# Windowed attention decode beside an MLP, one core: V streamed 256 columns at a time past masked P, exp written in 16-key runs, fewer idle products

## The chip, the core and the metric

The kernel runs on one core of a Trainium2 chip. The metric is the device time of one execution in microseconds (us); lower is better. The kernel before measures 216.69 us (median of 4 runs, 216.23 to 217.12). A profile's span is about 1.3 us shorter than the time of the same run.

## The reference, cut to what matters

One decoding step for 4 sequences: the output is the sum of the input, windowed attention over a cache, and a small MLP.

```python
# A: attention; 32 query heads, 16 kv heads, head width 128
W = min(4096, max(256, Sk // 4))                 # 2048 keys
q = (xn @ wq) ...                                # x is [4, 1, 576]
k, v = last W keys of k_cache, v_cache           # [4, 16, 2048, 128] each, bf16
p = softmax(q k^T * Dh**-0.5);  o = p v
attn = o @ wo                                    # wo [4096, 576]
# B: MLP
h  = gelu(layernorm(xn) @ w1);  x1 = xn + shift(h) @ w2
h2 = gelu(layernorm(x1) @ w3) @ w4               # w3 [576, 4608], w4 [4608, 576]
return x + attn + x1 + h2
```

K and V are 33.6 MB each, the weights 21.4 MB more. 88.49 MB have to come from HBM, and every byte of the cache is used once.

## The kernel before: the parts that matter

The program is written as lists of instructions for each engine with explicit semaphores. One queue issues all large loads in order: weights, 16 K pieces of 2 MB, 8 V pieces of 4 MB into four buffers, then wo, then w4 in five pieces. V piece 4 may be issued only when piece 0 has been used, and so on.

```python
v_free = [["hT1", "hs1", "h2_3"], ["h2_3"], [t_done(NC - 3)], [t_done(NC - 1)]]
for c in range(8):                               # V pieces
    add_dma([(vslot[q], ...)], ("v", q), [f"PV{c - 4}_3"] if b else v_free[q], KS + c)
ev_wo = add_dma(..., "wo", ["PV4_3"], KS + 8)
# w4: five pieces of 18, 9, 6, 2, 1 rows, waiting for PV5_3 (two) and PV6_3 (three)
```

After the K stage, exp computes P and writes its results one after the other to places that lie 64 elements apart (the layout of P itself stays the same in the change; only the order in which exp goes through it differs); P is transposed by products with selection matrices; VectorE multiplies it with a 0/1 mask into "pads" of 64 columns; and V is the *stationary* operand of each product:

```python
P_exp = P_sb.rearrange("p (i q t) -> p q t i", i=NI, q=4)     # innermost step: 64 elements
... activation(out=P_exp[:, q], in_=Sps[:, q, :].rearrange("p (t i) -> p t i", t=16), func=Exp, ...)

def pe_PV(c, j):                                 # a quarter of V piece c: 32 products of 64 columns
    for t in range(VQ):
        e.matmul(OTps, lhsT=vt[:, VQ * j + t, :], rhs=pads[:, j, t].rearrange("p h e -> p (h e)"), ...)
```

The V products stand in a loop of two passes (pieces 0 to 3, then 4 to 7), so that their instructions exist once. HOPS puts a jump at a chosen place inside the loop. IDLE puts products of zeros at three places of TensorE's program near the end: 3 before the permutation of the attention output, 7 after the wo products, 5 after the first w4 piece.

```python
IDLE = ((3, -2.7), (7, 0.5), (5, 20.5))
HOPS = (("K", 15), ("V", 5))
```

## Time and profile before

| | before |
|---|---|
| span of the profiled run | 215.7 us (that run took 217.06, the median is 216.69) |
| loads | 88.49 MB, DMA row full from slice 2 to 38 |
| TensorE busy | 153.5 us, mean granted clock 0.913 |
| one V piece on TensorE | 128 products, 3.9 us (full clock) to 5.4 us |
| one exp (128 x 512) | 2.76 us, four of them |
| last load landed | 211.59 us; end of the last product about 213.85 us |
| instruction fetches | 10, of 16 KB each |

DMA, the sixteen engines that move the loads, is the resource that is never free, and TensorE's chain after the wo load ends 2.3 us later than the last load. One line of the page counts the packets of the queue that fetches instructions (packets, MB, share of 16 engines):

```profile
q8 instruction: 10, 0.16, 0.3%
```

### The profile page before, as it was taken

How to read it: one execution, taken by the hardware profiler on the slowest of the kernel's cores; microseconds unless marked ns; L12 is line 12 of the kernel's file. 1: busy time of each engine (PE TensorE's matmuls, PEld its weight loads, DVE VectorE, ACT ScalarE, POOL GpSimd, SP SyncE). 2: the span in 40 equal slices, each digit the busy share in tenths (PEclk: the TensorE clock that was granted, in tenths of full speed). 3: DMA queues.
4: the chain of work that ended last, by engine and by line, in shares of the span. 5: the costliest groups of instructions: out<-in, count | busy, mean ns of one | idle time of the engine just before them, and what ended most of it. 6: DMA issues, size and time to landing. Idle time of an engine off the chain costs nothing. (4 is left out here: it accounts for less than half of the span.)

```text
span 215.7 us, 5968 instructions
## 1 busy us (share of the span) xinstructions
PE 153.5 (71%) x2688; PEld 118.5 (55%) x2691; DVE 104.4 (48%) x160; ACT 67.9 (31%) x74; POOL 15.5 (7%) x55
## 2 busy tenths in 40 slices
PE   0048499999999999999993009597566718380996
PEld 0023176777888788877882003587555718370553
DVE  0242522676666667666665111999679716110000
ACT  2001205655566666665565882000000000000000
POOL 8200000710000000000000000000000000000000
PEclk9999969999999999999999556999799967888599
DMA  7999999999999999999999999999999999999970
GB/s 292 402 404 462 437 407 425 422 427 422 428 434 425 422 434 425 433 428 425 441 431 444 431 437 428 425 434 422 437 416 444 413 456 413 447 410 429 405 317 5
DMA packets 5152, 88.68 MB, mean 411 GB/s; under 512 B 600, under 2 KB 740, under 8 KB 1300
## 3 DMA queue, kind: packets, MB, share of 16 engines
q1 hardware_dynamic: 5124, 88.49, 96.2%
q8 instruction: 10, 0.16, 0.3%
q14 instruction: 2, 0.02, 0.0%
q10 hardware_dynamic: 16, 0.01, 0.0%
HBM read 88.49 MB, written 0.00 MB: 410 GB/s over the span
## 5 line engine op out<-in xcount | busy, mean ns | idle before, releaser
L365 DVE COPY kt<-ps 128x1024 bf16<-128x1024 bf16 x80 | 52.3, 687 | 27.4 <-PE ps L358 27.2
L358 PE MATMUL ps<-perm_bf,ring 128*128 128x128 bf16 x1024 | 62.4, 219 | 1.6 <-PEq L607 0.6
L358 PEld LDWEIGHTS ps<-perm_bf,ring 128*128 128x128 bf16 x1024 | 57.5, 98 | 10.9 <-issue 10.8
L364 ACT ACTIVATE kt<-ps 128x1024 bf16<-128x1024 bf16 x48 | 49.1, 1024 | 31.1 <-PE ps L358 29.8
L436 DVE TENSOR_TENSOR kt<-PT,mU_bf 128x2048 bf16<-128x2048 bf16 x32 | 37.1, 1217 | 10.3 <-PE ps L447 10.1
L447 PE MATMUL ps<-kt,ring 128*128 128x64 bf16 x512 | 20.2, 211 | 14.5 <-PEq L607 10.2
L447 PEld LDWEIGHTS ps<-kt,ring 128*128 128x128 bf16 x512 | 19.7, 110 | 14.9 <-issue 14.9
L584 ACT ACTIVATE out_sb<-ps 4x288 bf16<-4x288 f32 x1 | 0.4, 402 | 79.6 <-PE ps L465 79.6
L447 PE MATMUL ps<-kt,w 128*128 128x64 bf16 x512 | 16.3, 193 | 7.0 <-PEq L607 5.8
L447 PEld LDWEIGHTS ps<-kt,w 128*128 128x128 bf16 x512 | 15.5, 98 | 7.8 <-issue 7.4
L372 PE MATMUL ps<-kt,Qs 128*32 128x512 bf16 x272 | 17.8, 382 | 1.4 <-PEq L607 1.4
L411 PE MATMUL ps<-kt,sel 128*128 128x512 bf16 x16 | 5.5, 516 | 12.2 <-ACT kt L403 12.2
L465 PE MATMUL ps<-w,ORT 128*4 128x288 bf16 x64 | 6.6, 392 | 5.9 <-DMA w<-in_A_wo_dram 5.9
L411 PEld LDWEIGHTS ps<-kt,sel 128*128 128x128 bf16 x16 | 1.9, 124 | 15.8 <-ACT kt L403 12.7
L393 POOL COPY Qs<-Qpad 128x128 bf16<-128x128 bf16 x16 | 4.6, 296 | 81.8 <-PE ps L372 67.4
L294 PE MATMUL ps<-ident_bf,xn_bf 4*128 4x4 bf16 x8 | 0.6, 170 | 13.7 <-DVE ragsrc L288 13.7
L583 DVE CAST out_sb<-ps 4x288 bf16<-4x288 f32 x1 | 0.4, 445 | 20.2 <-PE ps L465 20.2
L403 ACT ACTIVATE kt<-ps,negb 128x512 bf16<-128x512 f32 x4 | 9.4, 2702 | 2.6 <-DVE negb L400 2.6
L372 PEld LDWEIGHTS ps<-kt,Qs 128*32 128x32 bf16 x272 | 5.7, 95 | 6.8 <-issue 1.5
L465 PEld LDWEIGHTS ps<-w,ORT 128*4 128x4 bf16 x64 | 3.9, 115 | 8.4 <-issue 6.0
L294 PEld LDWEIGHTS ps<-ident_bf,xn_bf 4*128 4x128 bf16 x8 | 0.4, 112 | 13.8 <-issue 11.4
L278 ACT ACTIVATE sd<-mv 4x1 f32<-4x1 f32 x3 | 0.6, 202 | 16.2 <-DVE mv L276 16.2
(108 smaller groups left out, 81.2 us busy)
## 6 DMA issues: line engine op xcount, KB each, us to landing
ring<-in_A_k_cache_dram SPq DMA_DIRECT2D x16, 2048.0 KB, 14.4
w<-in_A_v_cache_dram SPq DMA_DIRECT2D x4, 4096.0 KB, 22.0
ring<-in_A_v_cache_dram SPq DMA_DIRECT2D x4, 4096.0 KB, 29.9
w<-in_B_w_dram SPq DMA_DIRECT2D x1, 4608.0 KB, 24.0
w<-in_A_wo_dram SPq DMA_DIRECT2D x1, 4608.0 KB, 34.0
kt<-in_A_wq_dram SPq DMA_DIRECT2D x1, 4096.0 KB, 13.1
w<-in_B_w_dram SPq DMA_DIRECT2D x1, 2592.0 KB, 33.8
w<-in_B_w_dram SPq DMA_DIRECT2D x3, 576.0 KB, 14.1
```

The lines of the kernel that those rows point to most:

```text
L278: add("act", lambda e: e.activation(out=sd[:, idx:idx + 1], in_=mv[:, idx, 1:2], func=ACTF.Sqrt, bias=EPS, scale=1.0), waits=[f"{tag}_mv"] ...
L294: e.transpose(XTps[idx][:, r, :], v[:, r, :], ident_bf[0:B, 0:B])
L358: ins = e.transpose(tb[n % 4][:, t, :], slot_t(c)[:, 8 * k + t, :], perm_bf[:])
L364: return "act", lambda e: e.activation(out=ktbuf[:, n % 16], in_=tb[n % 4], func=ACTF.Copy)
L365: return "dve", lambda e: e.tensor_copy(out=ktbuf[:, n % 16], in_=tb[n % 4])
L372: ins = e.matmul(Sps[32 * u:32 * u + 32, q, :].rearrange("p (t i) -> p t i", t=16), lhsT=Qs[:, c % NPOS, 32 * u:32 * u + 32], rhs=ktgrp[:, ...
L393: P(lambda e, c=c, cc=cc: e.tensor_copy(out=Qs[:, c % NPOS, :], in_=Qpad_t[:, 128 * cc:128 * cc + 128]), waits=["qT", "qs_zero"] + ([f"SC{ ...
L403: add("act", lambda e, q=q: e.activation(out=P_exp[:, q], in_=Sps[:, q, :].rearrange("p (t i) -> p t i", t=16), func=ACTF.Exp, bias=negb[: ...
L411: ins = e.matmul(ps[:, 4 + g, :].rearrange("p (q t) -> p q t", q=4), lhsT=sel[:, g // 2, g % 2, i, :], rhs=P_v[:, i], start=(i == 0), stop ...
L436: return lambda e: e.tensor_tensor(out=pads[:, j], in0=PTv[:, b, q, VQ * j:VQ * (j + 1), :].unsqueeze(2).to_broadcast([128, VQ, 32, 2]), i ...
L447: ins = e.matmul(OTps, lhsT=vt[:, VQ * j + t, :], rhs=pads[:, j, t].rearrange("p h e -> p (h e)"), start=(q == 0 and j == 0 and t == 0), s ...
L465: return e.matmul(ACC[h], lhsT=lhsT, rhs=rhs, start=start, stop=stop, tile_position=(0, 32 * h), skip_group_check=True)
```

## The change

Its intent is to give TensorE longer products in the V stage, which have less overhead and keep its clock up, and then to do without most of the idle products. Now masked P is the stationary operand (two pads side by side: 128 columns) and two V tiles of 128 columns move past it. Half of each 128 x 256 result is meaningless; the two diagonal blocks are copied out to fp32 and summed by products with a folding matrix. exp writes 16 keys next to each other. (The last lines of this diff tell the code in short.)

```diff
-IDLE = ((3, -2.7), (7, 0.5), (5, 20.5))
-HOPS = (("K", 15), ("V", 5))
+IDLE = ((3, -2.7),)
+HOPS = (("K", 15), ("V", 11))
-        P_exp = P_sb.rearrange("p (i q t) -> p q t i", i=NI, q=4)
+        P_exp = P_sb.rearrange("p (i q t) -> p q i t", i=NI, q=4)
-   activation(out=P_exp[:, q], in_=Sps[:, q, :].rearrange("p (t i) -> p t i", t=16), func=ACTF.Exp,
+   activation(out=P_exp[:, q], in_=Sps[:, q, :].rearrange("p (t i) -> p i t", t=16), func=ACTF.Exp,
...
-                for t in range(VQ):
-                    ins = e.matmul(OTps, lhsT=vt[:, VQ * j + t, :], rhs=pads[:, j, t].rearrange("p h e -> p (h e)"), ...)
+                for t in range(0, VQ, 2):
+                    t0 = (VQ * j + t) * Dh
+                    ins = e.matmul(Ops, lhsT=pads[:, j, t:t + 2].rearrange("p t h e -> p (t h e)"), rhs=vslot[q][:, t0:t0 + 2 * Dh], ...)
...
-   after piece 3 and 7: OTn[:, cols] = OTps * rinvB[:, cols]                      (VectorE)
+   after piece 3 and 7: Ov[0:64, b] = Ops[0:64, 0:128]       (VectorE)
+                        Ov[64:128, b] = Ops[64:128, 128:256] (ScalarE)
+   def pe_fold: for b in 0, 1: OTps[:, 64*b:64*b+64] = Ov[:, b, :]^T fold_f       (TensorE, fp32)
+   OTn = OTps * rinvB                                                             (VectorE)
```

More of the change, by code (lines that the diff above doesn't have):

```diff
@@ L132, in bass_parallel_sum__sliding_block_cached__mixer_s_mlp__decode_kernel @@
         OTn = sb("OTn", [128, 128], BF16)
+        Ov = sb("Ov", [128, 2, 128], FP32)
+        fold_f = sb("fold_f", [128, 64], FP32)
         OTy = sb("OTy", [128, B, 32], BF16)
@@ L143, in bass_parallel_sum__sliding_block_cached__mixer_s_mlp__decode_kernel @@
         rinvps = ps[:, 3, 0:128]
-        OTps = ps[:, 2, 256:320]
+        Ops = ps[:, 2, 256:512]
+        OTps = ps[:, 2, 128:256]
         Qps = [ps[:, 4 + k, :] for k in range(2)]
@@ L217, in bass_parallel_sum__sliding_block_cached__mixer_s_mlp__decode_kernel @@
             waits=["ident_f"], sig="mU", key=-8)
+        add("dve", lambda e: e.tensor_reduce(out=fold_f[:], in_=ident_f[:].rearrange("p (x j) -> p j x", x=2), axis=AX.X, op=ALU.add),
+            waits=["ident_f"], sig="fold_f", key=-7.9)
         P(lambda e: e.memset(sel_t[:], 0.0), waits=["qTp"], sig="sel_zero", key=3.5)
@@ L402, in bass_parallel_sum__sliding_block_cached__mixer_s_mlp__decode_kernel @@
         for q in range(4):
-            add("act", lambda e, q=q: e.activation(out=P_exp[:, q], in_=Sps[:, q, :].rearrange("p (t i) -> p t i", t=16), func=ACTF.Exp,
+            add("act", lambda e, q=q: e.activation(out=P_exp[:, q], in_=Sps[:, q, :].rearrange("p (t i) -> p i t", t=16), func=ACTF.Exp,
                                                    bias=negb[:, 0:1], scale=scale, accum_out=rs4[:, q:q + 1]),
@@ L441, in pe_PV @@
             q = c % 4
-            vt = vslot[q].rearrange("p (t d) -> p t d", t=VT)
             def f(e):
                 ins = None
-                for t in range(VQ):
-                    ins = e.matmul(OTps, lhsT=vt[:, VQ * j + t, :], rhs=pads[:, j, t].rearrange("p h e -> p (h e)"),
-                                   start=(q == 0 and j == 0 and t == 0), stop=(q == 3 and j == 3 and t == VQ - 1))
+                for t in range(0, VQ, 2):
+                    t0 = (VQ * j + t) * Dh
+                    ins = e.matmul(Ops, lhsT=pads[:, j, t:t + 2].rearrange("p t h e -> p (t h e)"), rhs=vslot[q][:, t0:t0 + 2 * Dh],
+                                   start=(q == 0 and j == 0 and t == 0), stop=(q == 3 and j == 3 and t == VQ - 2))
                 return ins
@@ L455, in bass_parallel_sum__sliding_block_cached__mixer_s_mlp__decode_kernel, with pe_fold @@
                     inc=[(tok("pad"), 1)], key=KV + 2 * c + 0.2 * j)
-                add("pe", pe_PV(c, j), waits=[take("pad")] + ([take(("v", q), 16)] if j == 0 else []) + ([take("otn")] if j == 0 and q == 0 else []),
+                add("pe", pe_PV(c, j), waits=[take("pad")] + ([take(("v", q), 16)] if j == 0 else []) + ([take("otn", 2)] if j == 0 and q == 0 else []),
                     sig=f"PV{c}_{j}", key=KV + 2 * c + 0.2 * j, loop=("V", b))
             if q == 3:
-                cols = slice(64 * b, 64 * b + 64)
-                add("dve", lambda e, cols=cols: e.tensor_tensor(out=OTn[:, cols], in0=OTps, in1=rinvB[:, cols], op=ALU.mult),
-                    waits=["rinvB", f"PV{c}_3"], sig="OTn1" if b else None, inc=[] if b else [(tok("otn"), 1)], key=KV + 2 * c + 2.5)
+                for x, eng in enumerate(("dve", "act")):
+                    o_, i_ = Ov[64 * x:64 * x + 64, b, :], Ops[64 * x:64 * x + 64, Dh * x:Dh * x + Dh]
+                    add(eng, (lambda e, o_=o_, i_=i_: e.activation(out=o_, in_=i_, func=ACTF.Copy)) if x else (lambda e, o_=o_, i_=i_: e.tensor_copy(out=o_, in_=i_)),
+                        waits=[f"PV{c}_3"], sig=f"Ov{x}" if b else None, inc=[] if b else [(tok("otn"), 1)], key=KV + 2 * c + 2.5)
+        def pe_fold(e):
+            ins = None
+            for b in range(2):
+                ins = e.matmul(OTps[:, 64 * b:64 * b + 64], lhsT=Ov[:, b, :], rhs=fold_f[:], start=True, stop=True)
+            return ins
+        add("pe", pe_fold, waits=["Ov0", "Ov1", "fold_f"], sig="OTp", key=KT - 4)
+        add("dve", lambda e: e.tensor_tensor(out=OTn[:], in0=OTps, in1=rinvB[:], op=ALU.mult), waits=["rinvB", "OTp"], sig="OTn1", key=KT - 3.5)
         def acc_mm(e, h, lhsT, rhs, start=False, stop=False):
@@ L552, in bass_parallel_sum__sliding_block_cached__mixer_s_mlp__decode_kernel @@
             add("pe", pe_h2(r), waits=["x1nT", "qT", "qs0", "qs1", ev_wq[1]] if r == 4 else [ev_w3], sig=None if r == 2 else f"h2_{r}",
-                inc=[(tok("otn"), 1)] if r == 2 else [], key=-9 + n)
+                inc=[(tok("otn"), 2)] if r == 2 else [], key=-9 + n)
         for k in range(3):
```

## The prediction

> **What bounds the kernel now.** I read the page first: the granted clock and the DMA row of the 40 slices.
>
> ```profile
> PEclk9999969999999999999999556999799967888599
> DMA  7999999999999999999999999999999999999970
> ```
>
> The sixteen DMA engines are full from the second slice to the 38th, while TensorE's clock is cut in places (the 5s) with no dent in the DMA row. 88.49 MB at about 430 GB/s is 206 us of the 215.7 us span. So nearly everything the engines do lies beside the stream of loads, and a part of the change can pay only where the stream has a hole or after it ends. Next, the chain that ended last (start us, us, what):
>
> ```profile
> 165.09 34.05 DMA w<-in_A_wo_dram
> 199.13 0.14 issue
> 199.27 7.16 PE ps L465 x68
> 206.43 0.16 issue
> 206.59 1.46 PE ps L471 x6
> 208.04 2.30 PE ps L465 x36
> 210.34 1.18 PE ps L471 x5
> 211.53 2.35 PE ps L465 x36
> 213.87 0.43 DVE out_sb L583
> ```
>
> The wo load lands at 199.13 after queueing for 34 us; from there it is TensorE alone: the wo products (L465 x68), 7 idle products (L471), the first w4 products, 5 idle ones, the rest, the copy out. It never waits for a w4 load. What the loads do meanwhile, in one-microsecond windows (stretch, length, busy of PE, PEld, DVE, ACT, POOL, clock, DMA share, GB/s):
>
> ```profile
> 209.00:210.00 1.00, 1.00 (x20) 0.72 (x18) 0.00 (x0) 0.00 (x0) 0.00 (x0) 1.00 0.47 167
> 210.00:211.00 1.00, 1.00 (x10) 0.40 (x7) 0.00 (x0) 0.00 (x0) 0.00 (x0) 1.00 0.06 24
> 211.00:212.00 1.00, 1.00 (x13) 0.44 (x13) 0.00 (x0) 0.00 (x0) 0.00 (x0) 1.00 0.01 3
> ```
>
> A share of 0.06 is one engine of sixteen: fifteen are done by about 210.2, one goes on to 211.6. The landing records say the same: the five w4 pieces are complete at 205.3, 208.4, 210.5, 211.2 and 211.6, each held up about 1.3 us by its one last engine. That engine is not late in V's last piece; it falls behind inside the wo load, when a 16 KB instruction fetch (starting at 195.8, 1.1 us long) is served. So two floors lie close together: TensorE's chain and, 2.3 us under it, the last landing.
>
> The V stage, from the timeline (start us, us, engine, line, what) and the page's groups:
>
> ```profile
> 121.34 2.76 ACT L403 ACTIVATE kt<-ps,negb 128x512 bf16<-128x512 f32 x1
> 137.20 4.11 PE L447 MATMUL ps<-kt,w 128*128 128x64 bf16 x128 [2.59 <-PEq L607]
> 161.16 3.89 PE L447 MATMUL ps<-kt,w 128*128 128x64 bf16 x128 [0.41 <-PEq L607]
> 187.05 5.44 PE L447 MATMUL ps<-kt,ring 128*128 128x64 bf16 x128 [4.40 <-PEq L607]
> L411 PE MATMUL ps<-kt,sel 128*128 128x512 bf16 x16 | 5.5, 516 | 12.2 <-ACT kt L403 12.2
> ```
>
> One V piece (128 pairs of weight load and 64-column product) takes 3.89 us at full clock, 30 ns a pair, and 5.44 us with the clock partly at half. The pieces land 9.7 us apart (138.4, 148.1, ..., 186.9), so TensorE has 4 to 6 us to spare in each.
>
> **What the Trainium skill says.** *TensorE: Matmul & The Clock Gate*, "Back-to-back issue gap", gives N/1.2 ns cold and N/2.4 + 2.5 ns warm for N moving columns. The trace agrees: the L411 weight loads (512 columns) lie 0.43 us apart at half clock and about 0.22 after it. Same page, Part 1: a free-running 3.4 us activity window sets the clock. The clock records here change on a 3.413 us grid, and every window with at most 1.26 us of matmul is followed by half clock, those of this stage with 1.63 or more by a full one. *SBUF — State Buffer*, "Specifications": 16-byte lines that want at least two hits each; exp, which writes single bf16 128 bytes apart, takes 2.7 us for 512 elements, where the copy of 512 columns at L420 takes 0.74. *Runtime: NRT & Kernel Launch*, "Instruction fetch mechanics": 16 KiB fetches by DMA, 128 KiB held by TensorE. The page lists 10 such packets, 0.16 MB, which agrees.
>
> **The change, part by part.**
> 1. *V as the moving operand.* 64 products of 256 columns replace 128 of 64. From L411, 256 columns cost about 0.108 us warm and 0.213 cold, so a piece takes 64 x 0.108 = 6.9 us warm and 13.6 wholly cold, against 3.9 and 5.4. TensorE's V work grows from 36.5 to about 55 us. In the first half it replaces the mask products of VectorE (L436, 1.217 us a quarter) as the pace, at 1.73 us a quarter; in the second half it fits the 9.7 us between landings. All of this is beside the loads.
> 2. *exp in 16-key runs.* Four exps drop from 2.7 to perhaps 0.9 us: V work starts about 6 us earlier (near 131 instead of 137.2). Hidden as well. It helps keep the releases early: the first four pieces end near 138, 145, 152 and 159, and the V loads that wait for them would be needed by the queue at 148, 158, 167 and 177.
> 3. *Tail of V.* Piece 7 lands at 186.9. Warm, it ends at 194; with one cold window, 195.7. Then two copies out of PSUM (about 0.3 us side by side), fp32 fold (0.4, from the fp32 product at L427: 0.38 for two), the scaling, transpose, permutation and copy: before 1.2 us, now about 2.1. Ready at 196.1 to 197.8, still ahead of wo at 199.13. Cost on the path: 0.
> 4. *Idle products.* 1.46 + 1.18 us and about 0.2 of issue gaps leave the chain: TensorE would end at 211.1 instead of 213.87, 2.8 us earlier. If the busier V stage keeps the clock up, the wo products (now at half clock: 103 ns each against 66 for the same shape after) save 2 us more.
> 5. *The floor.* The last w4 landing at 211.6, plus 0.14 for the wait (as after wo) and about 0.3 for the last two products, gives 212.05: only 1.8 us of that can be had while one engine is late by 1.3.
> 6. *Fewer instructions.* TensorE's program shrinks from 1229 to 963 static matmuls, with their weight loads 532 instructions, two 256-instruction blocks of fetch. Two of the four fetches inside the V loop go (and stalls put down to "issue" of 1.1, 2.6 and 1.7 us there). Each fetch delays one DMA engine; following the landings, different engines were hit. If the fetch near the end falls on an engine that is early, the last landing moves to about 210.3 and TensorE's 211.1 becomes the end.
>
> Sum: -1.8 us if the late engine stays, -2.8 to -3.1 if it goes. I can't tell which and take half of each, then give back 0.1 for the chance of a cold clock: -2.2 from 216.33 gives 214.1.
>
> **Rivals.**
> *TensorE becomes V's bound.* At half clock a piece needs 13.6 us of the 9.7 there are; the loads would starve and each late piece cost 4 us. For it: gaps of 2.7 us before each late piece can fall into one activity window. Against it: 16 cold products take 3.4 us, the other 48 another 5.2, together 8.6, under 9.7. If it did happen on two pieces: 222 or more.
> *The V tail passes wo.* It has 1.3 to 3 us of slack; a further 2 us of cold clock or a fetch stall before the fold would eat it, and the time would be 215 to 216.
> *Without idle products TensorE goes cold among the w4 pieces.* It now waits for landings; 18 products at 103 instead of 66 ns and a slow start cost 0.7 to 1: about 215.3.
> *Transfers hide all of it.* This is the floor of step 5, 214.5; for nothing at all to be gained the last landing would have to move back by 1.8 us, and the same bytes stream through the same queue.
>
> **Range and chances.** 212.9 would need both the early last landing and a warm clock; 215.6 covers the cold tail and the 0.4% spread of the runs before. Faster by 2% means under 212.0, below either floor: 5%. Slower by 2% means starved loads: 2%. Predicted 214.1, 8 in 10 between 213.0 and 215.6.
>
> **What would show it.** The DMA row stays full to the 38th slice. V products in groups of 64 per piece, about 6.9 us each, and TensorE at 170 us or more of busy time. exp near 1 us. wo still ends the wait before L479 (the old L465), near 199. The chain then holds no L471 after wo but ends in a w4 landing or an unbroken row of products. The instruction queue shows 8 packets. I am wrong if a V load is issued late enough to leave a hole in the DMA row, if the chain runs through the V products or the fold, or if exp has not become faster (that would cost no time, only show step 2 wrong).

## The result, and the profile after

The changed kernel takes 213.93 us (median of 4 runs, 213.86 to 213.98); the ratio to before is 0.9872 with a 95% interval of 0.9846 to 0.9899. (A ratio here is the mean time of one kernel's fast runs over that of the other's of the same rounds, so it is not quite the ratio of the medians.) The prediction of 214.1 was 0.2 us off, and "within 2%" was right.

From the page of the changed kernel, the granted clock and the DMA row of the 40 slices, and the queue of instruction fetches:

```profile
PEclk9999958999999999999999679999999999969999
DMA  7999999999999999999999999999999999999993
q8 instruction: 8, 0.13, 0.2%
```

The loads are as dense as before and end a slice-fraction earlier; TensorE's clock is now up nearly everywhere; there are two fetches fewer. The chain that ended last (start us, us, what):

```profile
184.71 24.68 DMA ring<-in_B_w_dram
209.39 0.04 issue
209.43 1.42 PE ps L479 x18
210.85 0.43 DVE out_sb L597
```

Before, the chain after wo was TensorE's own, product after product. Now it runs through the landing of w4's third piece at 209.39; TensorE has finished what it could and waits. The last loads in one-microsecond windows, columns as in the prediction:

```profile
209.00:210.00 1.00, 0.57 (x10) 0.43 (x12) 0.00 (x0) 0.00 (x0) 0.00 (x0) 1.00 0.35 126
210.00:211.00 1.00, 0.81 (x12) 0.20 (x8) 0.16 (x1) 0.13 (x1) 0.00 (x0) 1.00 0.00 0
```

Against 0.47 and 0.06 before: the single engine that went on alone until 211.6 is gone. The landing records (the trace holds, for each load, the times at which the sixteen DMA engines finished their parts) say the same: the last two of the sixteen finish 0.26 us apart (1.31 before), and the last landing is at 210.47 instead of 211.59.

The V stage from the timeline (start us, us, engine, line, what):

```profile
120.15 0.68 ACT L408 ACTIVATE kt<-ps,negb 128x512 bf16<-128x512 f32 x1
130.22 14.13 PE L452 MATMUL ps<-w,kt 128*128 128x256 bf16 x128 [2.51 <-PEq L621]
177.53 7.15 PE L452 MATMUL ps<-ring,kt 128*128 128x256 bf16 x64 [2.57 <-PEq L621]
187.24 8.56 PE L452 MATMUL ps<-ring,kt 128*128 128x256 bf16 x64 [2.56 <-PEq L621]
198.23 4.09 PE L479 MATMUL ps<-w,ORT 128*4 128x288 bf16 x64 [0.38 <-DVE ORT L499]
```

exp is four times as fast, the stage starts 7 us earlier (130.2 against 137.2), a piece takes 7.15 us instead of 3.9, and the last one 8.56 because one 3.4 us clock window from 186.8 on is at half speed. The wo products run at full clock: 4.09 us instead of 6.58. Note the last line's bracket: they wait for the attention output (ORT), 0.2 us after wo itself has landed at 198.01.

So two different things happened at the end: TensorE's chain became shorter than the loads, and the loads themselves ended 1.1 us earlier. The experiments take them apart.

### The profile page after: what moved, and what is told of

Same layout as the page of the kernel before. It is cut to its first block, busy times and chain, and to the rows that moved or that the text cites. A ratio compares the mean times of both kernels' runs of the same rounds, so it can differ in the third digit from the quotient of the medians.

```text
span 212.7 us, 4936 instructions
## 1 busy us (share of the span) xinstructions
PE 169.3 (80%) x2171; PEld 131.9 (62%) x2171; DVE 106.6 (50%) x162; ACT 61.6 (29%) x76; POOL 15.4 (7%) x55
## 5 line engine op out<-in xcount | busy, mean ns | idle before, releaser
L441 DVE TENSOR_TENSOR kt<-PT,mU_bf 128x2048 bf16<-128x2048 bf16 x32 | 38.7, 1223 | 17.9 <-PE ps L452 17.9
L452 PE MATMUL ps<-ring,kt 128*128 128x256 bf16 x256 | 29.8, 280 | 5.1 <-PEq L621 5.1
L452 PE MATMUL ps<-w,kt 128*128 128x256 bf16 x256 | 28.4, 272 | 4.8 <-PEq L621 4.8
L452 PEld LDWEIGHTS ps<-ring,kt 128*128 128x128 bf16 x256 | 25.6, 100 | 9.2 <-issue 5.6
L452 PEld LDWEIGHTS ps<-w,kt 128*128 128x128 bf16 x256 | 24.8, 98 | 8.3 <-issue 5.5
L466 ACT ACTIVATE Ov<-ps 64x128 f32<-64x128 f32 x2 | 0.5, 272 | 68.2 <-PE ps L452 68.2
L560 PE MATMUL ps<-w,x1nT 128*32 128x387 bf16 (+7 forms) x90 | 5.8, 400 | 2.7 <-DMA w<-in_B_w_dram 2.5
L560 PEld LDWEIGHTS ps<-w,x1nT 128*32 128x32 bf16 x90 | 4.5, 124 | 3.9 <-DMA w<-in_B_w_dram 2.6
L466 DVE COPY Ov<-ps 64x128 f32<-64x128 f32 x2 | 0.6, 283 | 10.4 <-PE ps L452 10.4
L479 PE MATMUL ps<-w,h2T_sb 128*4 128x288 bf16 x54 | 3.6, 286 | 2.1 <-DMA w<-in_B_w_dram 2.1
```

Of the source, the lines that this page charges most:

```text
L441: return lambda e: e.tensor_tensor(out=pads[:, j], in0=PTv[:, b, q, VQ * j:VQ * (j + 1), :].unsqueeze(2).to_broadcast([128, VQ, 32, 2]), i ...
L452: ins = e.matmul(Ops, lhsT=pads[:, j, t:t + 2].rearrange("p t h e -> p (t h e)"), rhs=vslot[q][:, t0:t0 + 2 * Dh], start=(q == 0 and j == ...
L466: add(eng, (lambda e, o_=o_, i_=i_: e.activation(out=o_, in_=i_, func=ACTF.Copy)) if x else (lambda e, o_=o_, i_=i_: e.tensor_copy(out=o_, ...
L479: return e.matmul(ACC[h], lhsT=lhsT, rhs=rhs, start=start, stop=stop, tile_position=(0, 32 * h), skip_group_check=True)
L560: ins = e.matmul(H2ps[k][32 * g:32 * g + 32, :].rearrange("p (x c) -> p x c", c=9)[:, :, off:off + cnt], lhsT=x_, rhs=w[:, base_:base_ + 1 ...
```

## The experiments

Twelve kernels ran, each beside runs of the kernel before on the same chip. "Gap" is the time between the last two engines in the landing records of the last w4 piece; fetches are the packets of the instruction queue.

| run | time us (median, range) | ratio to before | fetches | last landing us | gap us |
|---|---|---|---|---|---|
| before | 216.69 (216.23 to 217.12) | 1 | 10 | 211.59 | 1.31 |
| changed | 213.93 (213.86 to 213.98) | 0.9872 | 8 | 210.47 | 0.26 |
| e1 before, less idle | 215.20 (215.09 to 215.28) | 0.9934 | 10 | 211.65 | 0.95 |
| e2 changed, old idle | 214.22 (213.74 to 214.95) | 0.9896 | 8 | 210.39 | 0.12 |
| e3 before, new exp | 216.52 (216.01 to 217.39) | 1.0005 | 10 | 211.67 | 1.11 |
| e4 V and fold alone | 217.12 (215.79 to 217.78) | 1.0023 | 8 | 212.29 | 0.98 |
| e5 changed, old exp | 215.14 (214.14 to 217.13) | 0.9926 | 8 | 213.13 | 0.27 |
| e6 before, less idle, half a block added | 215.25 (215.04 to 215.28) | 0.9920 | 11 | 211.76 | 0.07 |
| e7 changed, half a block added | 215.28 (214.90 to 215.53) | 0.9929 | 9 | 211.39 | 0.91 |
| e8 changed, V 25% longer | 217.89 (216.03 to 218.14) | 1.0021 | 8 | 210.31 | 0.01 |
| e9 before, less idle, half of V's products | 213.94 (213.90 to 214.05) | 0.9863 | 8 | 210.54 | 0.25 |
| e10 changed, jump at 5 | 214.10 (213.92 to 214.18) | 0.9868 | 8 | 210.67 | 0.09 |
| e11 changed, no idle | 213.88 (213.80 to 213.98) | 0.9859 | 8 | 210.48 | 0.15 |
| e12 changed, two blocks added | 215.24 (215.11 to 215.40) | 0.9942 | 10 | 211.79 | 0.16 |

### e1: only the idle products taken out of the kernel before

```diff
-IDLE = ((3, -2.7), (7, 0.5), (5, 20.5))
+IDLE = ((3, -2.7),)
```

> The kernel before with only the 12 idle products taken out (3 stay). Theory (the last w4 landing is the floor, and it is late because an instruction fetch holds up one DMA engine inside the wo load): V and its fetches are as before, so the last landing stays near 211.6, the chain ends in a wait for it, span about 213.9, time 1.7 to 2.0 us under before. Rival (only TensorE's chain counts): 2.8 us under before, chain without a DMA wait after wo.

215.20 us, ratio 0.9934. The chain that ended last:

```profile
183.72 26.84 DMA ring<-in_B_w_dram
210.56 0.04 issue
210.60 1.43 PE ps L465 x18
212.03 0.43 DVE out_sb L583
```

It ends in a landing, at 210.56 for the piece that took 209.39 in the changed kernel. The last landing is 211.65 with the gap of nearly 1 us, and the span is 213.9, as the theory had it. The gain in time is 1.4 us, somewhat under the 1.7 expected. The rival's 2.8 us did not come. Counted from the run that was traced (217.06), on which the sum was worked out, the gain is 1.9 us. So taking out the idle products alone leads to the floor set by the late engine, and the rest of the gain, 1.3 us, must come from elsewhere. This kernel's runs also lie within 0.2 us of each other, where before spreads over 1.6 us in the same rounds. That the spread of before is the state of the clock under the wo products, which no longer shows once the landings set the end, is argued and not shown.

### e2: the idle products put back into the changed kernel

```diff
-IDLE = ((3, -2.7),)
+IDLE = ((3, -2.7), (7, 0.5), (5, 20.5))
```

> The changed kernel with the 7 and 5 idle products put back. Theory: the wo products run at full clock and end near 202.8, the idle products then fall into waits for w4 landings (204.2, 207.3, 209.4) and cost under 0.3 us: within 0.3 us of the changed kernel. Rival (the idle products cost what they last, 2.6 us): 1.5 to 2.6 us over the changed kernel.

214.22 us in the median: three runs at 213.7 to 213.9, three at 214.6 to 214.95. The profiled one (213.9) is of the first kind; TensorE's timeline shows why the idle products then cost nothing:

```profile
202.67 1.69 PE L485 MATMUL ps<-zeros_bf 128*128 128x512 bf16 x7
204.29 2.37 PE L479 MATMUL ps<-w,h2T_sb 128*4 128x288 bf16 x36
206.59 1.25 PE L485 MATMUL ps<-zeros_bf 128*128 128x512 bf16 x5
207.77 1.27 PE L479 MATMUL ps<-w,h2T_sb 128*4 128x288 bf16 x18
209.35 1.38 PE L479 MATMUL ps<-ring,h2T_sb 128*4 128x288 bf16 x18 [0.31 <-DMA ring<-in_B_w_dram]
```

They fill the time until the next landing (204.1, 207.2, 209.3). In the other three runs they cost up to 1 us; no trace was taken of those, and that the wo products then met a half-speed window is only argued. In the traces of e1 and e2, idle products cost no more than what exceeds the wait that they lie in.

### e3: only exp's new order in the kernel before

```diff
-P_exp = P_sb.rearrange("p (i q t) -> p q t i", i=NI, q=4)
+P_exp = P_sb.rearrange("p (i q t) -> p q i t", i=NI, q=4)
-   in_=Sps[:, q, :].rearrange("p (t i) -> p t i", t=16)
+   in_=Sps[:, q, :].rearrange("p (t i) -> p i t", t=16)
```

> The kernel before with only exp's new write order. Theory: exp falls from 2.7 to 0.7 us each, V starts some 6 us earlier, all of it beside the loads: time within 0.4 us of before, unless the earlier end of V's first half moves an instruction fetch. Rival (V's start matters to the releases and so to the stream): 1 us or more faster.

Ratio 1.0005: nothing, although exp takes 0.69 us and V starts at 131.3 instead of 137.2. With pieces of 4 us the V buffers are free in good time either way.

### e4 and e5: exp's old order in the changed kernel

e4 is the changed kernel with exp's two lines and IDLE as before (V and fold alone are new); e5 has only exp's two lines as before.

> The changed kernel with the old idle products and the old order of exp's writes: only V as moving operand and the fold are new. Theory: the gain comes with V's new form (two fetches fewer, so no late DMA engine, and a clock that stays up for the wo products): span under 213.6, within 0.5 us of the changed kernel, although V starts 6 us later. Rival (V's new form costs on the path, since TensorE has 7 instead of 4 us of work per piece): slower than before.

> The changed kernel with exp's old write order (so the V stage starts about 7 us later) and its few idle products kept. Theory formed on the run with V alone: with the slower 7.15 us pieces the release of the first V buffer comes near 145, too close to 146 to 148 where the queue runs dry, so every later landing is 1 to 2 us late: 215 to 216.5, a dip in the DMA row near 147 to 152. Rival (the run with V alone lost to its idle products, and exp's speed is hidden as the prediction said): within 0.3 us of the changed kernel.

e4 came out at 217.12 us, not under 214.5: my theory for it failed, and e5 was made to tell its idle products from exp. e5 has no idle products to blame and takes 215.14 us, 1.2 over the changed kernel, with a wide spread (214.14 to 217.13). Here is the window from 145 to 149 us, first in the changed kernel and then in e5 (columns as before; the last two are DMA share and GB/s):

```profile
145.00:149.00 4.00, 4.00 (x40) 3.57 (x38) 2.96 (x3) 0.00 (x0) 0.00 (x0) 1.00 0.98 418
```

```profile
145.00:149.00 4.00, 4.00 (x39) 3.57 (x38) 2.96 (x3) 0.00 (x0) 0.00 (x0) 1.00 0.70 238
```

There is the hole. In e5 the first V piece starts at 137.8 (130.2 in the changed kernel) and its 64 products, some of them in a half-speed window, end at 146.4; only then is piece 4 issued. The queue's last earlier load, piece 3, is finished by its first engine at 145.9 and by its last at 148.05, and the first packets of piece 4 start at 147.8, 1.3 us after the issue. Piece 4 lands at 160.17 instead of 157.96, and everything after it stays late: the last landing is 213.13. In e4 the issue comes at 145.0, before any engine is out of work, and with the same 1.3 us to the first packet it is still too late: the loss in that trace is 1.9 us at piece 4. By these numbers the issue has to come before about 144.6 (an estimate). The slower single runs of e4 and e5 are mostly those with a lower mean clock (0.937 against 0.952 and more in e4), as a slower first piece would make them; their holes were not traced. So exp's new order gains nothing by itself and is worth 1.2 us beside the longer V pieces: it buys back the time that they take from the release of the first buffer.

### e6 and e7: moving the fetch blocks

Both add 64 tiny products of zeros (128 instructions, half of a fetch block) at the start, where TensorE waits; e6 to e1's kernel, e7 to the changed one.

```diff
+        def pe_pad(e):
+            for _ in range(64):
+                ins = e.matmul(ps[:, 3, 0:16], lhsT=zeros_bf[:, 0:128], rhs=zeros_bf[:, 0:16], start=True, stop=True)
+            return ins
+        add("pe", pe_pad, waits=["zeros_bf"], sig=None, key=-50)
```

> The kernel before without the 12 idle products (215.2 us, last landing 211.65, a fetch at 195.85 inside the wo load), plus 64 tiny zero products (128 instructions, half a fetch block) early, where TensorE is idle: they only shift where the fetch blocks begin. Theory (the last landing is late because a fetch inside the wo load holds up one engine): if that fetch now comes at another time or hits another engine, the gap between the last two engines shrinks from 1 us to under 0.3 and the time falls to about 214.0; if a fetch stays there and hits a late engine, nothing changes. Rival (the lateness belongs to the 64-column form of V): gap and time stay whatever the fetches do.

> The changed kernel with 64 tiny zero products (128 instructions, half a fetch block) early, where TensorE is idle; they shift only where the fetch blocks begin. Theory (the last landing is late when a fetch is served inside the wo and w4 loads and hits an engine that is among the last): if a fetch starts between 187 and 207, the last engine trails the second last by about 1 us and the time is 1 us higher; if not, the gap stays under 0.3 us and the time within 0.3 us of the changed kernel. Rival (the lateness comes from V's form, not from fetches): gap and time as in the changed kernel whatever the fetches do.

e7 became slower by 1.35 us (215.28). Its ninth fetch starts at 208.4, and the gap between the last two engines is 0.27 us for w4's third piece and 0.97 and 0.91 for the two that finish after that fetch: cause and effect stand side by side in the records. This fetch lies outside the time (187 to 207) that I had given for it, so the theory was right on the mechanism and wrong on the place. e6 stayed at 215.25. It has 11 fetches: the one at 158.5 makes one engine late by 1.4 us from the next V landing (168.96) to the end, and the one at 197.2, inside the wo load, makes a second one late, which is why its gap at the end is only 0.07. It tells nothing against the rival by its time, but it showed something else: in e6 a fetch at 158.5 did the damage, in the kernel before one at 195.8, in e7 one at 208.4, and each of these was the *ninth* of its run. The changed kernel has eight.

### e9: a short program with V in its old form

e1's kernel, with every second V product left out, and the jump at 11. Its result is wrong; the comparison with the reference passed all the same, so that comparison says little about the V sums. What matters: V keeps its 64-column form, and the program is as short as the changed one's.

```diff
-                for t in range(VQ):
+                for t in range(0, VQ, 2):
                     ins = e.matmul(OTps, lhsT=vt[:, VQ * j + t, :], rhs=pads[:, j, t]..., 
```

> The kernel before without the 12 idle products, and with only every second of V's 64-column products (wrong result on purpose), the loop's jump placed as in the changed kernel: V keeps its old form, but the program is as short as the changed one, 961 static products, so 8 fetches are expected instead of 10. Theory (in all runs so far it is the ninth fetch that sets one of the last engines back; a program with only 8 has no late engine): last two landings within 0.3 us of each other, last landing near 210.5, time near 214.0. Rival (V as the moving operand, with its fuller clock, is what makes the landings early): gap of 1 us and more, last landing 211.6, time 215.2.

213.94 us, the time of the changed kernel. From its page:

```profile
PEclk9999969999999999999999655955965555567589
q8 instruction: 8, 0.13, 0.2%
```

The clock is at half speed for most of the V stage (mean 0.832), exp is slow, V is in its old form; but there are eight fetches, the gap is 0.25 us and the last landing is at 210.54. One of these eight (the seventh, at 192.4) lies inside the wo load and does no harm. That separates the number of fetches from the clock, from V's form, and from the time of the fetch; not from the amount of V work, which is halved too, and for that e12 is the test.

### e12: a long program with V in its new form

The changed kernel with 128 tiny products at the start and 128 more while exp runs: two fetch blocks.

```diff
+                for _ in range(128):
+                    ins = e.matmul(ps[0:4, bank, 0:16], lhsT=zeros_bf[:, 0:4], rhs=zeros_bf[:, 0:16], start=True, stop=True)
...
+        add("pe", pe_pad(3), waits=["zeros_bf"], sig=None, key=-50)
+        add("pe", pe_pad(7), sig=None, key=KS + 0.1)
```

> The changed kernel with 128 tiny zero products before the first transposes and 128 more while exp runs: 512 instructions, two whole fetch blocks, all in time TensorE has to spare, so the program fetches as often as the old one: 10 times. Theory (the ninth fetch sets back an engine that is among the last): the ninth now comes near 159, where in the changed kernel the seventh is; from V's next landings on the last engine trails the second last by 1.0 to 1.4 us, the last landing is 211.4 to 211.9, time 214.9 to 215.4. Rival (what counts is that the fetch falls inside the wo load, as the prediction put it): no fetch there, gap under 0.3 us, 213.9 as the changed kernel. A time above 215.6 would mean that the added products delay something else.

215.24 us. The ninth fetch starts at 159.6; V's piece 5 then lands with a gap of 1.36 us (0.27 in the changed kernel), the later loads keep it, and the last landing is at 211.79. (For the very last piece the table has 0.16, because the tenth fetch, at 209.65, makes a second engine late.) No fetch falls inside the wo load. The queue of fetches, and the last full microsecond of the loads with a DMA share of 0.07, about one engine of sixteen (0.00 in the changed kernel):

```profile
q8 instruction: 10, 0.16, 0.3%
210.00:211.00 1.00, 0.42 (x8) 0.33 (x10) 0.00 (x0) 0.00 (x0) 0.00 (x0) 1.00 0.07 24
```

The theory's numbers came true, and the version that the prediction had given (inside the wo load) is ruled out.

### e8: how much V work is free

A product of zeros after every four, 80 instead of 64 products per piece.

```diff
+                    if t // 2 % 4 == 0:
+                        e.matmul(ps[:, 3, 0:2 * Dh], lhsT=zeros_bf[:, 0:128], rhs=zeros_bf[:, 0:2 * Dh], start=True, stop=True)
```

> The changed kernel with 4 more 256-column products of zeros per quarter (80 instead of 64 per piece), results unchanged. Theory: a piece takes 8.7 to 9 us, still under the 9.7 between landings, but TensorE works without a pause from 130, so piece 7 ends near 200 instead of 195.8 and the wo products start near 202.5: 1 to 2 us over the changed kernel. Rival (anything under 9.7 us is free): within 0.3 us.

217.89 us, 4 us over the changed kernel, where I had expected 1 to 2. The landings are as early as ever (210.31), but TensorE works from 131.0 on without a pause and the wo products start late:

```profile
205.50 4.09 PE L481 MATMUL ps<-w,ORT 128*4 128x288 bf16 x64 [0.38 <-DVE ORT L501]
210.10 3.47 PE L481 MATMUL ps<-w,h2T_sb 128*4 128x288 bf16 x54
```

A piece takes 8.7 us, under the 9.7 between landings, and still it is too long: eight of them from 131.0 end at about 200.8 at best, and a half-speed window at the start and the copy between the passes brought it to 203.1. The limit is the sum from the start of V to wo's landing at 198.0, less some 2.4 us for fold and transposes. With a start at 130.2 that allows about 8.2 us for each piece (an estimate from these numbers), and the changed kernel uses 7.15.

### e10 and e11: the jump and the last idle products

e10 is the changed kernel with the jump back at 5; e11 has `IDLE = ()`.

> The changed kernel with the jump inside the V loop back at position 5 (it is 11 in the change). Theory: the jump only decides when a fetch of the loop is asked for, 8 fetches stay, and V has slack: within 0.3 us of the changed kernel. Rival: a stall on a fetch inside the first pass delays the release of the first V buffers, opens a hole in the stream, and costs over 0.5 us.

> The changed kernel without its last 3 idle products (before the permutation). Theory: they fill a wait of TensorE for VectorE (0.8 us) and cost at most 0.1 us; the end is the last landing: within 0.2 us of the changed kernel, or slower where the clock window then goes half speed under the wo products (up to 0.7 us, if their end passes the landing of the first w4 piece). Rival: they sit on the chain and 0.6 us is to be had.

214.10 and 213.88 us; against the changed kernel's 213.93 both are as expected. Neither part is worth anything that these runs could show. e11 is no faster than the change beyond the noise, and no run beat it; what is left is the stream itself.

## Why the prediction was right, point by point

- **The number.** 214.1 against 213.93 is closer than the working deserves. The two sums, 1.8 us if the late engine stays and 2.8 to 3.1 if it goes, were read from the trace of a run that took 217.06. Taken from that run they give 215.3 and 214.0 to 214.3, and the runs came close to both: 215.20 in e1, 213.93 in the change. The prediction took the mean of both outcomes, too little by 0.6 to 0.9 us for the one that came, from a median of 216.33, lower by 0.7 than the traced run. The two slips cancel, and that is luck; the two outcomes are not.
- **The bound.** Right. In all runs whose V buffers were released in time, the last landing was at 210.3 to 211.8, whatever TensorE, ScalarE or the clock did.
- **Step 4, the idle products.** The mechanism was right: they leave the chain, which then meets the landings. e1 isolates it: a span of 213.9, as the floor of step 5 said. In time it was 1.4 us against the median of its rounds and 1.9 against the traced run, where the sum had 1.8.
- **Step 5 and 6, the late engine.** The step named the cause, the right amount (a last landing near 210.3 or 211.6; measured 210.47 and 211.6) and the right two outcomes. I gave each one half, and the late engine went. e9 and e12 show that it is the length of TensorE's program that decides: six runs with nine fetches or more have the last landing at 211.4 to 211.8, six with eight and no hole in the stream have it at 210.3 to 210.7. Wrong was the place: "falls behind inside the wo load" is where it happened before, but not the condition, which is the ninth fetch wherever it falls. The landing records show what is different about the ninth. Across a fetch, the landings of one engine move back by 1.5 us against those of the other fifteen. In the kernel before, the fifth to eighth fetches met engines that were 1.5 to 2.0 us ahead of the last one, so nothing came of it; the ninth met one only 0.2 us ahead and left it 1.3 behind. In the other five runs with a ninth fetch the engine that it met was 0.2 to 0.6 us ahead and ended 0.9 to 1.4 behind the next. Why the ninth goes to such an engine while others are still 2 us ahead is not shown: the records carry no engine numbers. Nor are eight fetches a safeguard by themselves: e4 has eight and, after its hole, a gap of 0.98 us.
- **Steps 4 and 6, TensorE's side.** I had TensorE at 211.1 and needed a warm clock for the lowest times. In the changed kernel the wo products did run at full clock (4.09 us), but e9 at half clock is just as fast. The clock was not a part of the gain.
- **Step 1.** 6.9 us per piece was predicted, 7.15 measured; half of the pieces lie back to back from 130.2 to 158.3, the rest follow the landings, the last three with gaps of 1.9 to 2.6 us. "Beside the loads" held. But the sum of the pieces is nearer to the path than the 9.7 us per landing suggested: e8 shows the limit at about 8.2.
- **Step 2.** The direction was right and the effect of exp on its own is zero (e3). But "hidden as well" was not true of the change as a whole: with the longer pieces the earlier start is needed, and without it the change gives back 1.2 us (e5). My time for when the V loads "would be needed by the queue", 148, was the last engine's; the first engine is out of work at 145.9 and the first packet comes 1.3 us after the issue, so 145.0 (e4) and 146.4 (e5) were both too late.
- **Step 3.** Right to 0.4 us: the last piece ended at 195.8 with one half-speed window (195.7 predicted). The attention output was ready at 198.2, just after wo (198.01, itself 1.1 us earlier than before). So the slack that I gave as 1.3 to 3 us was gone, and the sign "wo still ends the wait before L479, near 199" did not come; the end did not move only because the first w4 piece lands at 204.2.
- **The rivals.** "TensorE becomes V's bound" did not happen, and e8 shows what it would look like. "The V tail passes wo" did happen, by 0.2 us, and cost nothing, for the reason just given. "TensorE goes cold among the w4 pieces" did not happen: 36 of those products took 2.37 us, 66 ns each, as before. "The transfers hide all of it" happened for the half that concerns the idle products, at the size given.

## What to carry to other kernels

Where a stream of loads fills the DMA engines, ask of every change what it does to the last landing, and look at the engines one by one there: a DMA share of one sixteenth over the last microsecond is one late engine, and it can be late because of the instructions that are fetched through it. The length of a program then has a price: here one fetch, the ninth, cost 1.3 us. And two parts of a change can be worth nothing alone and something together: the faster exp only pays because the new V pieces are slower, so test parts inside the change as well as inside the kernel before.

## What the Trainium skill lacked or had wrong

- *Runtime: NRT & Kernel Launch*, "Instruction fetch mechanics", calls the cost of crossing a 16 KiB boundary mostly hidden. Here each fetch took 0.9 to 1.1 us beside a full DMA queue, and the ninth put one of the sixteen engines 0.9 to 1.4 us behind all others for the rest of the stream; with nine (e7) or ten (e12) fetches instead of eight the kernel took 1.3 us longer. Which engine a fetch is served by is on no page that I found.
- *TensorE: Matmul & The Clock Gate*, Part 1, has the clock fall after an idle window, and gives no amount of work that keeps it up. Here windows with 1.71 us (before, from 197.56), 1.34 us (changed, from 183.34) and 2.90 us (e9, from 139.23) of matmul in 3.41 were followed by half clock, so a window need not be idle. The limit that the prediction read from the V stage (1.26 us half, 1.63 full) does not carry over to these.
- *SBUF — State Buffer*, "Specifications", says that crossing lines costs, with no size: exp on 128 x 512 took 2.76 us with each bf16 in another line and 0.69 us with runs of 32 bytes (its reads of PSUM changed too, from neighbours to steps of 32 elements, so this is the sum of both).
